# A gated mix of a state-space scan and an MLP on one core: W1 read and summed twice, scan allowed into the output stage, full-size b2 rows, x loaded first

## The chip, the cores and the metric

The kernel runs on one core of a Trainium2 chip. A core has engines that run side by side, each with its own queue in program order: TensorE (PE, matrix products, whose results go to eight banks of PSUM), VectorE (DVE), ScalarE (ACT), GpSimd (POOL) and SyncE (SP). SP, ACT and POOL also issue transfers (DMA) between the chip's main memory and the on-chip SBUF. Engines wait for one another through semaphores. The time is that of one execution on the device in microseconds (us), lower is better. Several executions give a median; one of them was taken with the hardware profiler.

## The reference

For x of 2048 rows and 1024 columns in bf16 (S rows, D columns), with F = 3584 hidden columns:

```python
x = A_x
g = sigmoid((x * gate_w).sum(-1, keepdims=True))
# A: diagonal complex state space, P = 1024 states
dt = exp(log_dt); Lam_bar = exp(dt * Lam)
B_bar = ((Lam_bar - 1) / Lam)[:, None] * (B_re + 1j * B_im)
Bu = einsum("bld,pd->blp", x, B_bar)
for t in range(L): h = Lam_bar * h + Bu[:, t]
a = 2 * einsum("blp,dp->bld", h, C_re + 1j * C_im).real + x * Dskip
# B: MLP on the layer-normed x
y = layernorm(x)
b = gelu(y @ w1 + b1) @ w2 + b2
return g * a + (1 - g) * b
```

## The kernel before, in words

**Matrix products with seven multiplications.** Every large product is done on 2 by 2 blocks with seven block products instead of eight. The class `SG` (L836) holds one such *group*: `p1` to `p7` are its seven products, each written by `mm` (L819) as a run of matmuls of 128 by 128 stationary and 128 by 512 moving operands (L828 where a bank is started, L830 where it is added to). Four of the seven use sums or differences of blocks. These are fp16 or bf16 tiles that DVE makes beforehand with `dve_tt` (L881 and L882), always in sets of four additions. Banks of PSUM are taken in rings: two for `p1`, two for `p5`, three for `p6`, so a bank comes round again two or three groups later.

**Stages on PE, in this order.** First x and B are transposed on PE (`t_x`, `t_b`) or by a transposing DMA, and the *bu* stage multiplies x by B, some of it plainly (`bu_plain`), the rest in groups (`bu_group`). Results go to the buffer `US` in main memory. The gate and the row sums of x come from a product with two columns (`z_gate`, L1024, bank 7). They are written to memory and read back in another layout (`z_move`, L1043), and layernorm (`ln_stats`) follows. Then come the MLP stages, eight of them: m(Fh,c) multiplies half c of the rows by half Fh of W1 and ends in gelu, and b(Fh,c) multiplies this by half Fh of W2. Their order is m(0,0), b(0,0), m(0,1), b(0,1), m(1,1), b(1,1), m(1,0), b(1,0) (L1465). The results of b, times (1 - g), are stored to or added into the buffer `ACS` in memory. The last stage, y, takes eight state blocks of 256 rows one after another, multiplies each by C (`y_group`, L1437), adds what `ACS` holds and the Dskip term, and stores the output.

**W1.** `w1_prep` (L1219) brings one 256-column block of W1 into one of four slots. Each half of W1 is used by two m stages. At the first use (m(0,0) and m(1,1)) the raw block is read, 512 KB in rows of 512 bytes, DVE makes the four sums (L1236 to L1239), and POOL stores block and sums together, 896 KB, to the buffer `W1S` (L1241). At the second use this is read back (L1225), with no work for DVE.

**b2.** In the b stages with Fh = 0 each group has two more matmuls that add b2. One has a stationary operand of one row of ones, the other of two rows (+1 and -1), against rows of b2 held in `B2B`: `v_one`, `v_sgn`, `v_b2l`, `v_b2r`. They are the only matmuls that read the tile `stg`.

**The scan.** `ssm` (L1120) does one *unit*: four blocks of 128 states by 256 rows. There are sixteen units. Each reads from `US`, multiplies by a table of rotations (L1142), combines (L1145), scans (L1156) and turns back, all on DVE, and stores to `HS`. Its buffers are three slots in `SSM` and two temporaries. It has the lowest priority on DVE (50) and so fills what the stages on PE leave. Units 8 to 15 finish state blocks 0 to 7.

**The y stage.** `y_load` (L1417) loads a state block (L1421), the rows of `ACS` (L1431) and of x (L1432), and has DVE multiply x by Dskip (L1433) and add it, times the gate, to the rows of `ACS` (L1434). `y_prep` makes the sums of the state block; `fin` makes the output from the banks (L1453 and L1455). The blocks come in the order 4, 5, 6, 7, 0, 1, 2, 3 (`YORD`). The places `H0` (states), `AV` (rows of `ACS`), `XV` (x) and `DB` (Dskip) lie in `SSM`, in the scan's tables `TABR` and in what hidden activations (`HT`) and W2 (`W2Q`) leave free. In particular the first two states lie in `SSM` and the first four rows of `ACS` in `TABR`, which the scan uses until it ends.

**What sets the order.** All work is entered as tasks with a priority and with dependences found from the memory that they read and write. A planner (`_schedule_once`) plays the tasks with modelled durations and writes one fixed order for each engine. At run time each engine executes its order and waits by semaphore. A task that waits holds up everything behind it on its engine.

Of the kernel before, what the change touches and what calls it, by code (L numbers as in the profile page):

```python
# [419 lines left out]
def build(nc, A_x, A_Lambda_re, A_Lambda_im, A_B_re, A_B_im, A_C_re, A_C_im, A_log_dt, A_Dskip,  # L420
# [6 lines left out]
    CH = 512  # L427
# [18 lines left out]
    with es:  # L446
# [194 lines left out]
        def t_x(k, prio):  # L641
            bk = tbank()
            v = XNAT[k]

            def em(e, k=k, bk=bk):
                ins = None
                base = XNAT[k].ap
                for dt in range(DT):
                    src = AR.v(XOFF(k) + dt * 256, [(1, 128)]).ap
                    ins = e.transpose(V(PS16[bk], dt * 128, [(1, 128)]), src, V(IDENT, 0, [(1, 128)]))  # L650
                return ins
            g.add("pe", 0.06 * DT, prio, em, reads=[v, b_ident], writes=[b_ps[bk]], name="xT_T%d" % k)
            o = AR.v(xqo(0, 0) + k * 256, [(512, DT), (1, 128)])
            first_e.append(g.add("dve", 0.65, prio, lambda e: e.tensor_copy(o.ap, V(PS16[bk], 0, [(128, DT), (1, 128)])),
                                 reads=[b_ps[bk]], writes=[o, b_ps[bk]], name="xT_e%d" % k))

        def t_b(pt, prio):
            s = pt % 4
            for ri in range(2):
                bk = tbank()  # L660

                def em(e, ri=ri, bk=bk):
                    ins = None
                    for dt in range(DT):
                        src = AR.v(RX + s * 4096 + ri * 2048 + dt * 256, [(1, 128)]).ap
                        ins = e.transpose(V(PS16[bk], dt * 128, [(1, 128)]), src, V(IDENT, 0, [(1, 128)]))
                    return ins
                g.add("pe", 0.06 * DT, prio, em, reads=[BN[pt], b_ident], writes=[b_ps[bk]], name="bT%d.%d" % (pt, ri))
                o = AR.v(bqo(pt, 2 * ri), [(1, D)])
                first_a.append(g.add("act", c_act(D), prio, lambda e, o=o, bk=bk: e.activation(o.ap, V(PS16[bk], 0, [(1, D)]), AF.Copy),  # L670
                                     reads=[b_ps[bk]], writes=[o, b_ps[bk]], name="bTe%d.%d" % (pt, ri)))

        load_b(0, (-0.95, 0))
# [5 lines left out]
        for k in range(4):  # L679
            t_x(k, (-0.8, k))  # L680
        t_b(0, (-0.79, 0))
        bk0 = tbank()
        g.add("pe", 0.06, (-0.75, 0),
              lambda e: e.transpose(V(PS16[bk0], 0, [(1, NROW)]), V(STG, 0, [(1, 128)], npart=NROW), V(IDENT, 0, [(1, NROW)], npart=NROW)),
              reads=[b_stg, b_ident], writes=[b_ps[bk0]], name="cst_T", extra=[g.tasks[-2]])
        g.add("pool", 0.4, P0,
              lambda e: e.affine_select(V(STG, 0, [(1, 128)], npart=2), V(ONESF, 0, [(1, 128)], npart=2), [[0, 128]], ALU.is_equal, -1.0,
                                        base=0, channel_multiplier=1),
              reads=[b_ones], writes=[b_stg], name="signs").slack = 4.0
        v_one = View(V(STG, 0, [(1, 128)], npart=1), [b_stg])  # L690
        v_sgn = View(V(STG, 0, [(1, 128)], npart=2), [b_stg])
# [324 lines left out]
        b_zs = B("zs")  # L1016
# [26 lines left out]
        def z_move():  # L1043
            prio = (1.0, seq[0])

            def em_st(e):
                return [e.dma_start(out=ZS[r].rearrange("(c t) -> c t", c=NCH), in_=bass.AP(AR.h[F32], r * zrow + ZR // 4, [[32 * zrow, NCH], [1, CH]])) for r in range(2)]
            g.dma(prio, em_st, 2 * L * 4, sem("d_zst", True), reads=[zr], writes=[b_zs], name="zst", ndma=2, q="pool").slack = 0.5

            def em_ld(e):  # L1050
                return [e.dma_start(out=C(("Z", "SUM")[r], 0, NTT), in_=bass.AP(ZS.tensor, ZS.offset + r * L, [[1, 128], [128, NTT]]), allow_slow_non_contiguous=True) for r in range(2)]
            g.dma(prio, em_ld, 2 * L * 4, sem("d_zl"), reads=[b_zs], writes=[bc("Z%d" % k) for k in range(NTT)] + [bc("SUM%d" % k) for k in range(NTT)], name="zl", ndma=2)
# [15 lines left out]
        for c in range(2):  # L1068
            if c == 1:
                z_gate(0)  # L1070
            for pt in range(2):
                bu_plain(pt, c)
# [4 lines left out]
        for n, (pt, pr) in enumerate(order):  # L1077
# [3 lines left out]
            if (pt, pr) == (0, 1):  # L1081
                z_gate(1)
                z_move()
                x_sums(1, seq[0])
# [35 lines left out]
        def ssm(pg, q):  # L1120
            s = nxt("sb", NSB)
            so, MA, MB = SB0 + s * 4096, TM0, TM0 + 4096
# [59 lines left out]
        v_b2l = AR.v(B2B, [(1, 512)], npart=1)  # L1182
        v_b2r = AR.v(B2B + 1024, [(1, 512)], npart=2)
# [35 lines left out]
        def w1_prep(j, first, q, ex=()):  # L1219
# [20 lines left out]
            ov = AR.v(o0, [(1, 3584)])  # L1240
            g.dma((10.0, q), lambda e: e.dma_start(out=W1S[j], in_=ov.ap), 128 * 7168, ssem("w1s", s, True), reads=[ov], writes=[b_w1s[j]], name="w1s%d" % j, q="pool")  # L1241
# [85 lines left out]
        def b_group(Fh, c, tp):  # L1327
# [8 lines left out]
            if Fh == 0:  # L1336

                st["A11"], mv["B11"] = st["A11"] + [v_one], mv["B11"] + [v_b2l]
                st["S1"], mv["T1"] = st["S1"] + [v_sgn], mv["T1"] + [v_b2r]
# [32 lines left out]
        H0 = [SSM, SSM + 8192] + [HT + 8192 * i for i in range(4)] + [SSM, SSM + 8192]  # L1372
        YR = HT + 49152
        AV = [TABR + 4096 * i for i in range(4)] + [YR + 4096 * i for i in range(4)]
        XV = [SSM + 16384, YR + 16384, YR + 18432, HT + 43008, HT + 45056]
        DB = SSM + 18432
# [4 lines left out]
        YORD = (4, 5, 6, 7, 0, 1, 2, 3)  # L1381
# [35 lines left out]
        def y_load(yi):  # L1417
# [3 lines left out]
            g.dma((52.0, yi), lambda e: e.dma_start(out=o.ap, in_=HS[qb]), 2 * UE * 128 * 2, ssem("hg", yi), reads=[b_hs[pg][qb] for pg in range(PG)], writes=[o], name="hg%d" % yi,  # L1421
                  extra=pe_last if yi > 2 else ())
            if yi == 0:
                g.dma((51.0, 0), lambda e: e.dma_start(out=v_db.ap, in_=bass.AP(A_Dskip.tensor, A_Dskip.offset, [[0, 128], [1, D]])), 128 * D * 2, sem("d_dskb"), writes=[v_db], name="dskb")
            for t in range(2):
# [3 lines left out]
                xi = 0 if n < 4 else 1 + n % 4  # L1429
# [3 lines left out]
                g.add("dve", c_tt16(D), (52.0, n), lambda e, xv=xv: e.tensor_tensor(xv.ap, xv.ap, v_db.ap, ALU.mult), reads=[xv, v_db], writes=[xv], name="xd%d" % k)  # L1433
                g.add("dve", c_dve(D), (52.0, n, 1), lambda e, xv=xv, av=av, k=k: e.scalar_tensor_tensor(av.ap, xv.ap, C("G", k), av.ap, ALU.mult, ALU.add),  # L1434
                      reads=[xv, av, bc("G")], writes=[av], name="xa%d" % k)

        def y_group(yi):  # L1437
# [5 lines left out]
            su, s5 = AR.v(YU[yi % 2], [(1, 512)], F32), AR.v(AO + 16384, [(1, 512)], F32)  # L1443
# [23 lines left out]
        for (kind, Fh, c) in blocks:  # L1467
            if kind == "m":
                for j in range(NP2):
                    w1order.append((Fh * NP2 + j, (Fh, c) in ((0, 0), (1, 1))))  # L1470
# [37 lines left out]
        for n, it in enumerate(flat):  # L1508
# [4 lines left out]
            if (kind, Fh, c, x) == ("b", 1, 0, 3):  # L1513
                y_load(0)
                y_load(1)
# [39 lines left out]
            if n == 0:  # L1555
                def em_b2(e):
                    return [e.dma_start(out=AR.v(B2B, [(1, D)], npart=1).ap, in_=bass.AP(B_b2.tensor, B_b2.offset, [[0, 1], [1, D]])),
                            e.dma_start(out=AR.v(B2B + 1024, [(1, 512)], npart=1, p0=1).ap, in_=bass.AP(B_b2.tensor, B_b2.offset, [[0, 1], [1, 512]]))]
                g.dma((40.0, 0), em_b2, 4096, sem("d_b2b"), writes=[v_b2l, v_b2r], name="b2b", ndma=2)
# [6 lines left out]
            if last_of_block:  # L1566
                if nit is None:
                    prev.p4()
                else:
# [13 lines left out]
                    else:  # L1583
# [5 lines left out]
                        prev.p4()  # L1589
                    prev = None  # L1590
# [53 lines left out]
```

## Time and profile before

| | us |
|---|---|
| median of 4 executions | 575.82 |
| lowest, highest | 574.67, 577.54 |
| the profiled execution | 574.67 |
| its span, first to last instruction | 572.9 |
| PE busy in the span | 552.1 |
| DVE busy in the span | 511.7 |

A row of the profile names line, engine, operation, what is written and read with its shape, and a count. "L828 PE MATMUL ps<-ar" is a matmul of line 828 that reads the large SBUF tile `ar` and writes PSUM. In the views in order of time the first number is the start and the second the length, both in us; a bracket gives the idle time before it and what ended it. A matmul's length includes its passage through the array and overlaps the next one, so the distance between starts is what it costs. In the page a row of groups gives the busy time, the mean of one in ns, and the idle time before them. PEld is the loading of the stationary operand. The granted clock of PE is 0.998 in this execution.

### The profile page before, as it was taken

The numbers are of one execution on the slowest core, as the hardware profiler recorded it, in microseconds if no ns is written. First come the engines' busy times: TensorE is split into PE (matmuls) and PEld (weight loads), VectorE is DVE, ScalarE is ACT, GpSimd is POOL, SyncE is SP. The second block draws the span as 40 slices with busy tenths as digits, with TensorE's granted clock in tenths as the row PEclk, the third lists the DMA queues.
The fourth block names the chain that finished last, engine by engine and source line by source line (L and its number), as shares of the span: only waits on it lengthen the run. The fifth ranks groups of instructions, "written<-read, shape, count | busy, mean of one in ns | idle before, by whom it ended". The sixth has DMA issues, their size and how long they took to land.

```text
span 572.9 us, 7432 instructions
## 1 busy us (share of the span) xinstructions
PE 552.1 (96%) x2569; PEld 249.0 (43%) x2617; DVE 511.7 (89%) x865; ACT 279.6 (49%) x465; POOL 98.8 (17%) x159
## 2 busy tenths in 40 slices
PE   5899999999999999999999999999999999999994
PEld 4444444444334444444434444444444444444442
DVE  3899999999999999999999999999995878998652
ACT  2978999667652247662236673336662322111110
POOL 0024856630101010001211000210000210011000
PEclk9999999999999999999999999999999999999999
DMA  8995999889994766403878999899669999777501
GB/s 273 234 285 111 286 298 317 276 286 288 373 256 127 262 244 228 146 33 114 263 295 295 336 286 212 212 276 258 199 144 255 305 311 281 246 246 265 180 37 55
DMA packets 116675, 134.50 MB, mean 235 GB/s; under 512 B 70548, under 2 KB 92565, under 8 KB 115614
## 3 DMA queue, kind: packets, MB, share of 16 engines
q1 hardware_dynamic: 102548, 79.72, 50.1%
q0 software_dynamic: 13952, 54.29, 29.6%
q8 instruction: 20, 0.33, 0.2%
q14 instruction: 17, 0.14, 0.1%
q10 hardware_dynamic: 138, 0.02, 0.0%
HBM read 63.48 MB, written 54.80 MB: 206 GB/s over the span
## 4 chain that ended last, share of the span: by engine, by line
PE 82%; DVE 11%; issue 2%; ACT 2%; DMA 1%; SPq 0%; DVEq 0%; ACTq 0%
PE ps L830 57%; PE ps L828 24%; DVE ar L882 4%; DVE ar L1142 2%; DVE ar L1275 2%; DVE ar L1156 1%; DVE ar L1145 1%; DMA ar<-in_A_x_dram 1%; ACT ar L670 1%; PE ps L1033 1%; PE ps L650 0%; DVE ar L1357 0%; ACT ar L912 0%; ACT L720 0%; DVE ar L968 0%
## 5 line engine op out<-in xcount | busy, mean ns | idle before, releaser
L830 PE MATMUL ps<-ar 128*128 128x512 f16 (+1 forms) x1683 | 389.9, 379 | 4.1 <-DVE ar L1357 1.0
L830 PEld LDWEIGHTS ps<-ar 128*128 128x128 f16 (+1 forms) x1720 | 166.3, 98 | 207.2 <-issue 4.4
L828 PE MATMUL ps<-ar 128*128 128x512 bf16 (+1 forms) x741 | 181.7, 379 | 1.4 <-DVE ar L882 0.8
L882 DVE TENSOR_TENSOR ar<-ar 128x512 f16<-128x512 bf16 (+7 forms) x216 | 139.9, 686 | 8.0 <-PE ps L828 3.4
L828 PEld LDWEIGHTS ps<-ar 128*128 128x128 bf16 (+1 forms) x752 | 72.6, 98 | 90.2 <-DVE ar L882 3.5
L1156 DVE TENSOR_TENSOR_SCAN ar<-cst,init,ar 128x256 bf16<-128x256 f32 x128 | 88.0, 735 | 0.4
L846 ACT ACTIVATE ar<-ps 128x512 f32<-128x512 f32 x100 | 58.9, 593 | 48.2 <-PE ps L828 33.2
L1142 DVE TENSOR_TENSOR ar<-ar 128x2048 bf16<-128x2048 bf16 x64 | 77.2, 1219 | 0.0
L854 ACT ACTIVATE ps<-ps 128x512 f32<-128x512 f32 x66 | 38.5, 583 | 71.8 <-PE ps L828 65.2
L1271 ACT ACTIVATE ar<-ps,cst 128x512 bf16<-128x512 f32 x56 | 38.4, 686 | 25.9 <-PE ps L830 25.4
L847 ACT ACTIVATE ar<-ps,cst 128x512 f32<-128x512 f32 x32 | 22.0, 687 | 56.6 <-PE ps L828 35.8
L1354 ACT ACTIVATE ar<-ps,cst 128x512 f32<-128x512 f32 x32 | 22.0, 687 | 46.1 <-PE ps L830 46.1
L1277 ACT ACTIVATE ar<-ar,cst 128x512 bf16<-128x512 f32 x56 | 40.0, 715 | 8.5 <-DVE ar L1275 8.4
L1145 DVE TENSOR_TENSOR ar<-ar 128x1024 bf16<-128x1024 bf16 x64 | 42.4, 686 | 0.2
L1275 DVE TENSOR_TENSOR ar<-ps,ar 128x512 f32<-128x512 f32 x56 | 38.3, 684 | 2.7 <-PE ps L830 2.2
L897 POOL DMA_DIRECT2D scr_u<-ar x32 | 25.1, 785 | 52.0 <-ACT ar L912 17.8
L1357 DVE SCALAR_TENSOR_TENSOR ar<-ps,cst,ar 128x512 f32<-128x512 f32 x32 | 23.9, 748 | 11.2 <-PE ps L830 11.1
L1455 DVE SCALAR_TENSOR_TENSOR ar<-ps,cst,ar 128x512 bf16<-128x512 f32 x32 | 23.8, 748 | 9.7 <-PE ps L830 9.6
L1366 POOL DMA_DIRECT2D scr_ac<-ar x16 | 13.8, 881 | 81.2 <-issue 32.9
L1364 POOL DMA_DIRECT2D scr_ac<-ar x16 | 8.5, 532 | 100.6 <-DVE ar L882 47.7
L1462 POOL DMA_DIRECT2D out_dram<-ar x14 | 7.6, 544 | 83.4 <-DVE ar L1455 83.4
L1174 POOL DMA_DIRECT2D scr_h<-ar x16 | 9.6, 600 | 66.9 <-DVE ar L1145 66.7
(105 smaller groups left out, 261.8 us busy)
## 6 DMA issues: line engine op xcount, KB each, us to landing
scr_ac<-ar POOLq DMA_DIRECT2D x32, 512.0 KB, 7.6
scr_w<-ar POOLq DMA_DIRECT2D x14, 896.0 KB, 6.5
ar<-scr_w SPq DMA_DIRECT2D x14, 896.0 KB, 6.0
ar<-in_A_x_dram SPq DMA_DIRECT2D x32, 256.0 KB, 5.1
scr_u<-ar POOLq DMA_DIRECT2D x32, 256.0 KB, 4.8
ar<-scr_u SPq DMA_DIRECT2D x16, 512.0 KB, 5.7
scr_h<-ar POOLq DMA_DIRECT2D x16, 512.0 KB, 7.2
ar<-scr_ac SPq DMA_DIRECT2D x16, 512.0 KB, 7.3
```

The source lines that it names most:

```text
L828: ins = e.matmul(V(PS[bk], 0, [(1, n)]), st[i].ap, mv[i].ap, start=(i == 0), stop=(i == K - 1))
L830: ins = e.matmul(V(PS[bk], 0, [(1, n)]), st[i].ap, mv[i].ap, start=False, stop=(i == K - 1), skip_group_check=True)
L846: return e.activation(o.ap, V(PS[bk], 0, [(1, 512)]), AF.Copy)
L854: g.add("act", c_act(512), (pb[0], q - 2), lambda e: e.activation(V(PS[b], 0, [(1, 512)]), V(PS[a], 0, [(1, 512)]), AF.Copy), reads=[b_ps[ ...
L882: g.add("dve", c_tt16(n), (pb[0], q), lambda e: e.tensor_tensor(o.ap, a.ap, b.ap, op), reads=[a, b], writes=[o], name=nm, extra=ex).slack ...
L897: g.dma((1.0, q), lambda e: e.dma_start(out=US[pt // 4, :, 4 * pr:4 * pr + 4, r0:r0 + T], in_=evv.ap), 2 * 128 * CH * 2, ssem("us", 2 * ks ...
L1142: g.add("dve", c_tt16(UE), pri(i), lambda e: e.tensor_tensor(o.ap, a.ap, tbl.ap, ALU.mult), reads=[a, tbl], writes=[o], name=nm + tag)
L1145: g.add("dve", c_tt16(UE // 2), pri(i), lambda e: e.tensor_tensor(o.ap, a.ap, b.ap, op), reads=[a, b], writes=[o], name=nm + tag)
L1156: lambda e, pt=pt, ri=ri, vin=vin, go=go: e.tensor_tensor_scan(go.ap, Cb("R", pt, T), vin.ap, V(INIT, pt * 2 + ri, [(1, 1)]), ALU.mult, AL ...
L1271: g.add("act", c_act(512, ap_operands=1), (10.0, q + 1), lambda e: e.activation(o.ap, V(PS[bk], 0, [(1, 512)]), AF.Gelu_apprx_tanh, bias=C ...
L1275: g.add("dve", c_dve(512), (10.0, q - 2), lambda e: e.tensor_tensor(sv.ap, V(PS[bk], 0, [(1, 512)]), sv.ap, ALU.add), reads=[b_ps[bk], sv] ...
L1277: g.add("act", c_act(512, psum=False, ap_operands=1), (10.0, q + 3), lambda e: e.activation(o.ap, sv.ap, AF.Gelu_apprx_tanh, bias=C("B1", ...
```

## The change

- **x first.** The loads of x's first two blocks go out ahead of B's; B's real and imaginary halves are loaded by separate tasks (`load_b0`) between and behind the blocks of x. The transposes on PE follow the same order, in an order fixed by dependences, with banks of their own.
- **Full-size b2 rows.** The sign tile has 128 rows (row 0 is 1, the others -1), and `B2B` is cleared on POOL before b2 is loaded into its rows 0 and 1, so that the two matmuls of b2 have full-size operands.
- **The gate in halves.** `z_move` stores and reads back each half of the rows as soon as its `z_gate` is done.
- **W1.** Every use reads the raw block and makes the four sums; the store to `W1S` is gone.
- **Scan and y.** Units 13 and 15 use a buffer in the tables of the first eight units, and unit 14 the third slot, so that two slots of `SSM` come free after unit 12. `H0`, `AV`, `XV` and `DB` get new places. `YORD` becomes 4, 5, 6, 0, 1, 2, 3, 7. At the start of the last W2 group only the first state block and Dskip are loaded; the rows of `ACS` and x for the first block, and everything for the second, are entered after that group's last product. The Dskip work gets priority 49 (52 before), ahead of the scan. The intermediate `s5` gets two places in turn.

```diff
+        load_b0(0, A_B_re)
+        load_b0(1, A_B_im)
+        BN[0] = AR.v(RX, [(1, 2 * D)])
         for k in range(4):
             load_x(k, (-0.9, k))
...
+        t_x(0, (-0.8, 0), 7, [])
+        t_x(1, (-0.8, 1), 3, last_pe())
+        t_b(0, (-0.8, 2), (0,), (1, 2), last_pe())
+        t_x(2, (-0.8, 3), 0, last_pe())
+        t_x(3, (-0.8, 4), 7, last_pe())
+        t_b(0, (-0.79, 0), (1,), (1, 2), last_pe())
+        bk0 = 3
...
-              lambda e: e.affine_select(V(STG, 0, [(1, 128)], npart=2), V(ONESF, 0, [(1, 128)], npart=2), [[0, 128]], ALU.is_equal, -1.0,
+              lambda e: e.affine_select(V(STG, 0, [(1, 128)]), V(ONESF, 0, [(1, 128)]), [[0, 128]], ALU.is_equal, -1.0,
...
             if c == 1:
                 z_gate(0)
+                z_move(0)
...
         def ssm(pg, q):
-            s = nxt("sb", NSB)
-            so, MA, MB = SB0 + s * 4096, TM0, TM0 + 4096
+            un = pg * NQ + q
+            s = nxt("sb", NSB) if un < 13 else 2 + un % 2
+            so, MA, MB = (SB0 + s * 4096 if s < 3 else TABR + 4096), TM0, TM0 + 4096
...
-        v_b2l = AR.v(B2B, [(1, 512)], npart=1)
-        v_b2r = AR.v(B2B + 1024, [(1, 512)], npart=2)
+        v_b2l = AR.v(B2B, [(1, 512)])
+        v_b2r = AR.v(B2B + 1024, [(1, 512)])
+        v_b2 = AR.v(B2B, [(1, D)])
...
-            ov = AR.v(o0, [(1, 3584)])
-            g.dma((10.0, q), lambda e: e.dma_start(out=W1S[j], in_=ov.ap), 128 * 7168, ssem("w1s", s, True), reads=[ov], writes=[b_w1s[j]], name="w1s%d" % j, q="pool")
...
-                st["A11"], mv["B11"] = st["A11"] + [v_one], mv["B11"] + [v_b2l]
+                st["A11"], mv["B11"] = st["A11"] + [v_sgn], mv["B11"] + [v_b2l]
...
-        H0 = [SSM, SSM + 8192] + [HT + 8192 * i for i in range(4)] + [SSM, SSM + 8192]
         YR = HT + 49152
-        AV = [TABR + 4096 * i for i in range(4)] + [YR + 4096 * i for i in range(4)]
-        XV = [SSM + 16384, YR + 16384, YR + 18432, HT + 43008, HT + 45056]
-        DB = SSM + 18432
+        H0 = [SSM] + [HT + 8192 * i for i in range(4)] + [SSM, HT, HT + 8192]
+        AV = [YR + 4096 * i for i in range(4)] + [AO + 2048, AO + 10240, TABR + 8192, TABR + 12288]
+        XV = [TABR, YR + 16384, YR + 18432, HT + 43008, HT + 45056]
+        DB = B2B
...
-        YORD = (4, 5, 6, 7, 0, 1, 2, 3)
+        YORD = (4, 5, 6, 0, 1, 2, 3, 7)
...
-                    w1order.append((Fh * NP2 + j, (Fh, c) in ((0, 0), (1, 1))))
+                    w1order.append((Fh * NP2 + j, True))
...
             if (kind, Fh, c, x) == ("b", 1, 0, 3):
-                y_load(0)
-                y_load(1)
+                y_load(0, ())
...
+                g.add("pool", 0.8, (39.0, 0), lambda e: e.memset(v_b2.ap, 0.0), writes=[v_b2], name="b2z")
                 g.dma((40.0, 0), em_b2, 4096, sem("d_b2b"), writes=[v_b2l, v_b2r], name="b2b", ndma=2)
...
                         prev.p4()
+                        if nk == "y":
+                            y_load(0, (0, 1), False)
+                            y_load(1)
```

## The prediction

> **What bounds the kernel now.** I began with the page's sums and its 40 slices (14.3 us each; a digit is the busy share in tenths).
>
> ```profile
> PE 552.1 (96%) x2569; PEld 249.0 (43%) x2617; DVE 511.7 (89%) x865; ACT 279.6 (49%) x465; POOL 98.8 (17%) x159
> PE   5899999999999999999999999999999999999994
> DVE  3899999999999999999999999999995878998652
> ```
>
> PE is full from the third slice to the last but one, and DVE nearly so until slice 30: PE sets the end, with DVE close behind. What can be won is time in which PE stands or steps slowly. In PE's timeline I took starts against starts: a 512-column matmul normally follows the last by 0.216 us (2,321 of 2,568 steps; a step of 0.43 is one record missing). The longer steps lie in three places.
>
> First the beginning, PE's timeline and then ACT's:
>
> ```profile
> 5.51 1.03 PE L650 MATMUL ps<-ident,ar 128*128 128x128 bf16 x8 [5.51 <-DMA ar<-in_A_x_dram]
> 7.05 2.85 PE L650 MATMUL ps<-ident,ar 128*128 128x128 bf16 x24 [0.50 <-DMA ar<-in_A_x_dram]
> 9.81 1.63 PE L666 MATMUL ps<-ident,ar 128*128 128x128 bf16 x16
> 11.94 0.21 PE L684 MATMUL ps<-ident,stg 76*128 76x76 bf16 x1 [0.50 <-ACT ar L670]
> 12.20 1.67 PE L828 MATMUL ps<-ar 128*128 128x512 bf16 x7
> ...
> 23.30 1.89 PE L1033 MATMUL ps<-ar,gwc 128*2 128x512 bf16 x16 [1.42 <-DVE ar L768]
> ```
> ```profile
> 10.86 1.94 ACT L670 ACTIVATE ar<-ps 128x1024 bf16<-128x1024 bf16 x2 [6.06 <-PE ps L666]
> 22.09 1.06 ACT L670 ACTIVATE ar<-ps 128x1024 bf16<-128x1024 bf16 x1
> ```
>
> PE waits for x, whose loads stand behind both halves of B's first block; the first real product starts at 12.20. The wait before 23.30 is named DVE, but the gate's product takes bank 7, and ACT empties it until 23.15: ACT ends that wait.
>
> Second, one b2 product of the sixteen (start, length):
>
> ```profile
> 183.25 1.46 PE L828 MATMUL ps<-ar 128*128 128x512 bf16 x6
> 184.64 0.38 PE L828 MATMUL ps<-ar,stg 1*128 1x512 bf16 x1
> 184.96 1.25 PE L830 MATMUL ps<-ar 128*128 128x512 f16 x5
> ```
>
> The step into it is 0.312 us and out of it 0.317, not 0.216.
>
> Third, stalls by stage, from the table by stage (length; busy PE, PEld, DVE, ACT, POOL; clock; DMA share; GB/s). The rows are m(0,0), m(0,1), m(1,1), m(1,0), b(1,0), y:
>
> ```profile
> 120.80:163.80 43.00, 41.95 (x188) 17.87 (x190) 42.84 (x68) 30.15 (x49) 5.28 (x9) 1.00 0.99 307
> 207.80:252.00 44.20, 43.89 (x202) 19.91 (x204) 42.53 (x65) 29.90 (x49) 2.12 (x4) 1.00 0.52 187
> 294.00:342.00 48.00, 46.20 (x211) 20.45 (x213) 47.30 (x75) 30.68 (x50) 5.25 (x10) 1.00 0.95 301
> 383.00:430.00 47.00, 46.48 (x214) 20.96 (x216) 45.95 (x71) 31.43 (x52) 3.27 (x6) 1.00 0.79 204
> 430.00:467.50 37.50, 37.34 (x172) 17.00 (x174) 27.55 (x34) 11.47 (x17) 5.69 (x7) 1.00 1.09 285
> 467.50:566.60 99.10, 97.77 (x447) 44.32 (x453) 76.38 (x103) 14.79 (x25) 8.83 (x16) 1.00 0.62 204
> ```
>
> Summing PE's long steps (b2's own excess left out): 1.8 us in m(0,0), 0.2 in m(0,1), 2.1 in m(1,1), 0.5 in m(1,0), 0.5 elsewhere after 25 us, none in b(1,0) and y. The two expensive stages are those that make W1's sums, also W2's sums, at a DMA share near 1.
>
> **x first.** The queue SP issues in order, 0.4 to 0.5 us each; before, the first six landings were 3.7, 4.3 (B), 5.5, 7.0, 7.7, 8.3 (x). The order becomes x0, x1, B re, x2, x3, B im. Giving these the same landings: x0's transposes begin at 3.7; B re is turned at 5.6 and copied by ACT until 7.5, before only until 11.8; x3 lands 7.7, B im 8.3; B im turned by 9.1; the constants' transpose follows in bank 3 with no wait for ACT (0.5 before). First product at about 9.4: 2.8 earlier. From there ACT's copies (one second-long copy per half of each of three more B blocks, as before) run about 11 us to the gate: 20.4 against 23.3. The other B blocks landed at 12.4 and transposed x at 16.5, so neither holds it. Ends: -1.0 if B's later blocks set ACT's pace, -3.0 if all of it arrives; I take **-2.6**, near what the landings give. PE has no stall over 0.27 from 25 to 120, so the shift arrives.
>
> **Full-size b2 rows.** Sixteen products, 0.096 in and 0.101 out: 16 x 0.197 = **-3.15**, all on PE. The Trainium skill ("TensorE: Matmul & The Clock Gate", *LDWEIGHTS* and the table of *Why this matters for your kernels*) speaks against it: a weight load's time goes by its columns and not its rows, and one matmul of few rows takes as long as a full one. By that the gain is 0; the row shows each alone is not shorter (0.38 us), but the steps around it are longer. I take the row, and keep 0 for the high end. The cost: one memset on POOL (204 ns was measured for 128x128), some 40 us before its use; nothing.
>
> **The gate in halves.** Two stores of 0.6 more on POOL, two loads of 0.6 more on SP. Between 40 and 50 us POOL is a quarter busy (2.68 of 10); the first half moves to about 25 us, where x's loads are queued on SP and could stand behind its load by up to 2.6 us (the old transfer's wait). They were issued from 24.1 and are wanted for layernorm, not by PE before 73.9: 0. Layernorm's first half may start earlier; PE never waited for it: 0.
>
> **W1's sums again.** 14 blocks more, four DVE additions each. One set took 1.47 us from start to start (1.56 busy at 127.77): 14 x 1.47 = **20.6 us of DVE**, half in m(0,1), half in m(1,0), ahead of the scan in priority, so the scan is what moves. It ended at 426 with its last store issued at 429.2; it would end near 447 plus what b(1,0) itself asks (DVE 27.5 of 37.5), so about 460. The cover: 9.95 us of idle DVE in b(1,0), 22.7 in y. 10.7 us are left for y, and some 2 us of Dskip work done before 467 move there too: 12.7 of 22.7. Only the last state block comes from the last scan unit, and it is now used last, at about 550; the others end by 440. So capacity suffices; without own buffers and order the 10.7 would stand before y.
> What can't be hidden is lateness: DVE runs in order, and a set behind a scan multiply (1.22) is late by that much. The nearest rows are the stages that have sets: 1.8 and 2.1 against 0.2 and 0.5. As much again would be +3.2; but the worst waits there stood behind W2's sums (two of 3584 elements took 2.35 at 148.09) and behind L1357, not a set alone. I take **+1.4** (0 to +4).
>
> **W1's stores gone, second reads smaller.**
>
> ```profile
> scr_w<-ar POOLq DMA_DIRECT2D x14, 896.0 KB, 6.5
> ar<-scr_w SPq DMA_DIRECT2D x14, 896.0 KB, 6.0
> ar<-in_B_w_dram SPq DMA_DIRECT2D x14, 512.0 KB, 6.3
> ```
>
> The 25 MB of the first two rows become 7.3 MB; a read takes as long. In m(0,0) a load took 10.8 us at worst, and POOL stood 15.0 for one with stores behind it. What waits for a store is the next load into its slot, which waits for the products too, and those end later: **-0.5** (0 to -1.5), by less crowding.
>
> **Into y.** The x and partial-sum loads for the first y blocks go into W2's place, so not before W2's last products, from 460 on, where four loads were already under way by 441. With 7.3 to landing the first is there at about 472; its use is the y block's first output at 476. If it is late, PE feels it only when the block after next (12.1 us each) takes that bank again, at 491. Moved with these loads: nine issues on SP (0.5 each), past nothing but the third block's, and beside two 512 KB stores of the last W2 group. The second state block (7.6) finds its place free after that group's first product and is used at 480; the third goes out at 473 as its place comes free, is used at 491. **+0.4** (0 to +6).
>
> **Sum** against the profiled execution, 574.67 (572.9 span, 1.8 around it): -2.6 - 3.15 + 1.4 - 0.5 + 0.4 = -4.45, 570.2. The median of the four is 575.82, 1.15 higher: **571.4**. About 0.3% (1.7 us) is what a measurement of this kernel can tell from no change: faster begins at 574.1, slower at 577.5.
>
> **Rivals.**
> - *The second sums come late* (slower). Place: DVE in m(0,1) and m(1,0). Each set stops PE by a good part of a scan multiply, 0.6 us: 8.4 instead of 1.4, 578.4. Break-even with the 5.65 gained and 0.5 and 0.4 netted is 0.41 a set; slower by 0.3% from 0.53. For it: DVE has 0.2 to 1.7 us idle per such stage. Against: m(0,0) and m(1,1) paid 0.28 a set, all causes together.
> - *The start doesn't shift*: x first, but ACT and B's later blocks set the gate's time; -0.5 instead of -2.6, and the sums 2.0 instead of 1.4: 574.1. For it: ACT is busy 9.25 of 10 us from 20 to 30. Against: it idles 6.06 before 10.86.
> - *The crowding was the cause of the stalls*: stores gone, sums hidden; m(0,0) and m(1,1) lose 3 of 3.9: 567.5. For it: the DMA share 0.99 and 0.95 there. Against: the longest wait, 1.0 at 298.29, is put down to DVE.
> - *The switch to y stalls*: late loads hold DVE in order, the sums of the next state behind them; +6: 577.
>
> **How the numbers follow.** Forecast 0.60 (own range 568.5 to 573.8), late sums 0.14, no shift 0.10, crowding 0.11, switch 0.05. Faster: 0.60 + 0.11 and half of no shift, 0.76; same: half of no shift and a third of the two slow ones, 0.11; slower 0.13. Range: 567.5 takes in crowding; above, I stop at 577.0, which leaves out most of the late sums.
>
> **What would show it.** First real product near 9.4 and the gate near 20.4; steps around b2 of 0.216; L1241's stores gone and 56 more additions; scan ending about 455 to 465 with y's first outputs not late; PE stalls in m(0,1) and m(1,0) of about 1.4 more together. It is wrong if those reach 6 us, if y has gaps over 1 us, or if b2's steps stay at 0.31.

## The result: no difference that can be measured

The changed kernel takes 576.54 us (median of 35 runs, 570.92 to 582.44), the kernel before on the same calls 575.35 (56 runs). The ratio is 0.9997, with a 95% interval of 0.9982 to 1.0012. The forecast was 571.4, a clear gain. Ratios here compare fast executions only, while the medians take in all of a kernel's executions, so the two part where a kernel has many slow ones (`start_only` below most of all).

The profiled execution of the changed kernel took 577.18 us (span 575.4) against 574.67 (572.9): 2.5 more. Its page, engine sums and the slices (14.4 us each) of PE and DVE:

```profile
PE 550.3 (96%) x2569; PEld 251.1 (44%) x2617; DVE 529.7 (92%) x921; ACT 278.5 (48%) x465; POOL 89.7 (16%) x148
PE   6999989889999999999999999999999999999985
DVE  4999889999999999999999999999999979999942
```

DVE has 18.0 us more work in 56 more instructions, as the change adds it. It is now full from slice 34 to 38, where it was at 8, 9, 9, 8, 6 before. PE has 1.8 us less work, yet its slices 6, 8 and 9 have fallen from 9 to 8.

The two early gains arrived. PE's timeline after, at the start and around one b2 product (start, length):

```profile
3.57 1.89 PE L649 MATMUL ps<-ident,ar 128*128 128x128 bf16 x16 [3.57 <-DMA ar<-in_A_x_dram]
...
9.71 1.67 PE L839 MATMUL ps<-ar 128*128 128x512 bf16 x7 [0.53 <-DVE cst L704]
...
19.33 1.89 PE L1044 MATMUL ps<-ar,gwc 128*2 128x512 bf16 x16
...
184.14 1.46 PE L839 MATMUL ps<-ar 128*128 128x512 bf16 x6
185.44 0.38 PE L839 MATMUL ps<-ar,stg 128*128 128x512 bf16 x1
185.65 1.67 PE L841 MATMUL ps<-ar 128*128 128x512 f16 x7
```

The first product starts at 9.71 (12.20 before) and the gate's at 19.33 (23.30), with no wait ahead of it. The b2 product lies 0.22 from the one before and 0.21 from the one after, where it was 0.31 and 0.32.

What ate them is in PE's waits after (total, times, longest) and in PE's timeline at the places of the largest ones:

```profile
PE ps L841 <- ACT ar L857: 4.3, 2, 2.5
PE ps L839 <- DVE ar L893: 2.5, 4, 1.1
PE ps L839 <- DMA ar<-scr_h: 2.4, 1, 2.4
```
```profile
77.71 1.90 PE L841 MATMUL ps<-ar 128*128 128x512 bf16 x8 [2.54 <-ACT ar L857]
...
103.85 1.90 PE L841 MATMUL ps<-ar 128*128 128x512 bf16 x8 [1.77 <-ACT ar L857]
...
503.68 1.90 PE L839 MATMUL ps<-ar 128*128 128x512 f16 x8 [1.11 <-DVE ar L893]
...
551.17 3.51 PE L839 MATMUL ps<-ar 128*128 128x512 bf16 x8 [2.42 <-DMA ar<-scr_h]
```

Summed from PE's start-to-start steps in both traces, beside the terms of the forecast (us, after less before). A stall is here the part of a step over 0.216, so it is somewhat longer than the idle time in the brackets:

| where | forecast | measured |
|---|---|---|
| start, to the gate's product | -2.6 | -4.0 |
| sixteen b2 products | -3.15 | -3.15 |
| first products, 53 to 120 us: stalls 0.27 before, 4.66 after | 0 | +4.4 |
| sums made twice: m(0,1), m(1,0) | +1.4 | -0.1 |
| stores gone: m(0,0) +0.5, m(1,1) -1.8 | -0.5 | -1.3 |
| W2 blocks b(0,0), b(0,1) and b(1,1) | 0 | +0.8 |
| output stage y: stalls 4.4, half clock about 1.6 | +0.4 | +6.0 |
| sum | -4.45 | +2.65 |

The measured sum is 0.1 to 0.2 off the difference of the two profiled executions. The miss is 7.1 us. Two rows, the first products and the output stage, are 10.0 over their forecast; the others are together 2.9 better than theirs.

**The first products.** The wait at 77.71 begins at DVE. DVE's timeline after, then ACT's:

```profile
74.52 0.42 DVE L893 TENSOR_TENSOR ar<-ar 128x512 f16<-128x512 bf16 x1 [4.03 <-DMA ar<-in_A_B_im_dram]
74.86 0.69 DVE L979 TENSOR_TENSOR ar<-ar 128x512 bf16<-128x512 f32 x1
```
```profile
75.63 0.60 ACT L977 ACTIVATE ar<-ps 128x512 f32<-128x512 f32 x1 [2.96 <-PE ps L841]
```

DVE, which takes its work in order, stands 4.03 us for a sum of blocks of B, until the transposing load of B im has landed. Behind it stands an addition on a finished product (L979, until 75.55). ACT's wait is named PE, but the product had been done since 75.18: the wait instruction at the head of ACT's queue, begun at 71.84, was released at 75.56, by L979. Then come ACT's L977, L807 and the copy that PE needs (L857, until 77.66), and PE goes on at 77.71.

That load of B im was issued at 60.5 and landed at 74.5; the last one went out at 64.9 and landed at 80.7. Before the change the last pair landed at 72.3 and 74.7. In that time the packets take long on average: from 66 to 68 us the 256-byte packets of the transposing loads 66 ns and the 4 KB packets of the stores on POOL's queue 617, where means of 22 to 34 and 160 to 170 are seen in the quicker stretches around it. But the median stays at 18 and 173 ns. A few packets stand very long, and they end together: 19 packets of 256 bytes that began within 0.05 us of 65.46 took 1.20 to 1.23 us each, and fifteen of 4 KB that began from 67.8 to 68.3 all ended at 69.7 to 69.8. So the transfers stop for 1 to 2 us at a time more than they run slowly. The DMA engines count as busy all that time, for a fraction of the bytes.

The wait at 103.85 stands behind ACT, which waits 1.56 us for DVE and then loads the table for the tanh at 101.80 (1.28 us) ahead of the copy that PE needs.

**The last state block.** Views of after: DVE's timeline, POOL's, then the chain of work that ended last:

```profile
472.57 1.28 DVE L1453 SCALAR_TENSOR_TENSOR ar<-ar,cst 128x1024 f32<-128x1024 bf16 x1 [2.35 <-DMA ar<-scr_ac]
...
502.34 0.69 DVE L1163 TENSOR_TENSOR ar<-ar 128x1024 bf16<-128x1024 bf16 x1
...
536.29 0.69 DVE L1163 TENSOR_TENSOR ar<-ar 128x1024 bf16<-128x1024 bf16 x1
```
```profile
541.66 1.20 POOL L1481 DMA_DIRECT2D out_dram<-ar  x2 [9.96 <-DVE ar L1474]
542.85 0.54 POOL L1192 DMA_DIRECT2D scr_h<-ar  x1
```
```profile
542.85 3.36 DMA scr_h<-ar
546.26 4.86 DMA ar<-scr_h
```

The scan has the lowest priority on DVE. From 470 to 480 DVE stands 4.5 us in order for rows of `ACS` and x whose loads take 11 to 15 us, with the rest of the last unit behind it; this rest comes from 495.5 to 503.0. Its very last addition (L1163, 0.69 us long) comes 33 us later still, at 536.29. The store is ready at 537.0, then stands 5.9 us in POOL's queue behind two stores of the output, which wait for DVE too, goes out at 542.85, lands at 546.2; the load lands at 551.1, and PE has stood for 2.4 us. The windows of the output stage of after (length; busy PE, PEld, DVE, ACT, POOL; clock; DMA share; GB/s):

```profile
480.00:490.00 10.00, 9.80 (x46) 4.33 (x45) 9.96 (x15) 1.62 (x3) 0.57 (x1) 1.00 0.91 364
...
530.00:540.00 10.00, 9.95 (x47) 4.55 (x47) 10.00 (x15) 1.57 (x3) 0.98 (x2) 1.00 0.37 107
540.00:550.00 10.00, 8.70 (x40) 3.78 (x39) 7.45 (x11) 1.19 (x2) 2.26 (x5) 1.00 0.55 190
550.00:560.00 10.00, 8.78 (x33) 3.68 (x35) 4.00 (x6) 1.21 (x3) 0.43 (x1) 0.83 0.18 72
```

DVE is full from 480 to 540 and has room only from about 545 on, after the last addition was due. In the window of PE's wait the granted clock is 0.83: for some 3.4 us a matmul follows the last by 0.427 us, not 0.216.

### The profile page after: what moved, and what is told of

Its sections match the earlier page's. It is cut to its first block, busy times and chain, and to the rows that moved or that the text cites. A ratio compares the mean times of both kernels' runs of the same rounds, so it can differ in the third digit from the quotient of the medians.

```text
span 575.4 us, 7467 instructions
## 1 busy us (share of the span) xinstructions
PE 550.3 (96%) x2569; PEld 251.1 (44%) x2617; DVE 529.7 (92%) x921; ACT 278.5 (48%) x465; POOL 89.7 (16%) x148
## 4 chain that ended last, share of the span: by engine, by line
PE 72%; DVE 17%; DMA 5%; issue 4%; ACT 1%; POOL 0%; SPq 0%; DVEq 0%; ACTq 0%
PE ps L841 49%; PE ps L839 21%; DVE ar L893 5%; DMA ar<-in_A_x_dram 2%; DVE ar L1453 2%; DVE ar L1160 2%; DVE ar L1474 2%; DVE ar L1293 2%; DVE ar L1452 1%; DVE ar L1472 1%; DMA ar<-scr_h 1%; DVE ar L1163 1%; DMA ar<-in_A_B_re_dram 1%; PE ps L665 1%; DVE ar L1174 1%
## 5 line engine op out<-in xcount | busy, mean ns | idle before, releaser
L893 DVE TENSOR_TENSOR ar<-ar 128x512 f16<-128x512 bf16 (+8 forms) x272 | 161.8, 631 | 8.8 <-DMA ar<-in_A_B_im_dram 4.0
L857 ACT ACTIVATE ar<-ps 128x512 f32<-128x512 f32 x100 | 58.6, 593 | 50.9 <-PE ps L839 38.6
L1163 DVE TENSOR_TENSOR ar<-ar 128x1024 bf16<-128x1024 bf16 x64 | 43.0, 686 | 0.3
L1474 DVE SCALAR_TENSOR_TENSOR ar<-ps,cst,ar 128x512 bf16<-128x512 f32 x32 | 23.9, 749 | 9.8 <-PE ps L841 9.7
L1453 DVE SCALAR_TENSOR_TENSOR ar<-ar,cst 128x1024 f32<-128x1024 bf16 x16 | 20.2, 1281 | 2.4 <-DMA ar<-scr_ac 2.4
```

Of the source, the lines that this page charges most:

```text
L857: return e.activation(o.ap, V(PS[bk], 0, [(1, 512)]), AF.Copy)
L893: g.add("dve", c_tt16(n), (pb[0], q), lambda e: e.tensor_tensor(o.ap, a.ap, b.ap, op), reads=[a, b], writes=[o], name=nm, extra=ex).slack ...
L1163: g.add("dve", c_tt16(UE // 2), pri(i), lambda e: e.tensor_tensor(o.ap, a.ap, b.ap, op), reads=[a, b], writes=[o], name=nm + tag)
L1474: g.add("dve", c_dve(512), (10.0, q), lambda e: e.scalar_tensor_tensor(o.ap, V(PS[bk], 0, [(1, 512)]), C("G", k), a.ap, ALU.mult, ALU.add) ...
```

## The experiments

My theory after the result had three parts. The start's gain is lost to crowded transfers in the first 120 us, because an earlier start is planned into another order. The gate in halves adds to that. And DVE's shortage stands before the last state block. The rivals: x first or the b2 rows bring nothing; the second sums of W1 come late in the middle stages; the stalls have other causes, so that undoing a part moves nothing. Each kernel's orders are planned anew, so a part that is undone can also move transfers elsewhere. "Before" was 575.1 to 575.6 us on all these calls. Ratios are to it, with 95% intervals.

**1. The early gains alone.** `start_b2` is the kernel before with x first and the full-size b2 rows; `start_only` has x first alone, `b2_only` the rows alone.

> The kernel before with x loaded first and full-size b2 rows, nothing else. Theory A (both early gains are whole, and the other parts eat them): the gate's product at 19.3 us instead of 23.3 and the b2 steps at 0.216, so 575.4 - 4.0 - 3.15 = 568.3 us, 567 to 570. Rival R1 (the earlier start itself runs into B's transposing loads and the stalls from 50 to 130 us come with it): 571 to 575.

> The kernel before with x loaded first alone. Theory D (in this plan, four us earlier, the transfers of 73 to 105 us fall into a stretch of slow packets, as in the run of both early parts): a wait of some 8 us near 99 us and the half clock after it, 581.9 + 3.15 = 585 us, 581 to 588. If the b2 part has a share in it: 571 to 576.

> The kernel before with full-size b2 rows alone. Its plan of the engines' orders is otherwise that of the kernel before. Theory A: sixteen products lose 0.197 us each, 575.1 - 3.15 = 572.0 us, 571.3 to 572.7. Rival (the time returns as waits on DVE in m(1,1)): 573 to 575.

| kernel | median us (runs) | ratio |
|---|---|---|
| `start_b2` | 581.89 (10) | 1.0078 (1.0041 to 1.0115) |
| `start_only` | 582.99 (21) | 1.0073 (1.0048 to 1.0097) |
| `b2_only` | 573.28 (22) | 0.9974 (0.9956 to 0.9992) |

x first, which takes 4 us off the start, makes the kernel slower by 0.7%. `start_b2` came out above both of its expectations. Its PE waits, PE's timeline, and the windows around the place:

```profile
PE ps L841 <- ACT ps L865: 10.6, 2, 7.8
```
```profile
99.52 6.49 PE L841 MATMUL ps<-ar 128*128 128x512 f16 x16 [7.80 <-ACT ps L865]
```
```profile
90.00:95.00 5.00, 1.72 (x8) 0.59 (x6) 0.00 (x0) 1.63 (x3) 0.00 (x0) 1.00 1.31 124
95.00:100.00 5.00, 0.48 (x2) 0.21 (x3) 2.65 (x5) 2.66 (x6) 1.07 (x2) 0.51 1.10 160
100.00:105.00 5.00, 5.00 (x13) 1.69 (x12) 4.37 (x10) 3.67 (x7) 2.45 (x4) 0.50 1.18 221
```

At 90 to 95 us DVE and POOL do nothing, the DMA share is 1.31 and 124 GB/s move. In flight are, among others, two stores of u (issued 78.8 and 79.6, landed 91.4 and 97.3), the first W1 store (83.1, landed 100.3) and a transposing load of layernorm's result (78.6, landed 101.3). The 256-byte packets from 85 to 100 us take 82 ns on average (median 18). PE stands for 7.8 us; the clock is at half from 95.1 to 105.4, and PE works in the last 5.8 us of this. The rows alone bring 1.5 us by the ratio and 2.0 by the medians, of their 3.15: in their profile PE gained a wait of 1.7 us in y (behind ACT's L845) that the kernel before has not.

**2. Holding one group of loads.** `start_b2_hold` is `start_b2` with W1's first loads held until the transposing loads of layernorm's result have landed:

```
+        xl = [t for t in g.tasks if t.name.startswith('xnT0')]
         for _ in range(4):
-            w1_next(0)
+            w1_next(0, xl)
```

> The kernel before with x first and full-size b2 rows, as in the first run of these two, and W1's first loads held until layernorm's transposing loads have landed, so that W1's first store doesn't fall among them. Theory D: without that overlap the packets stay at their usual time, the 8 us wait near 99 us goes, 568 to 573. If the transposing loads and the stores of Bu alone bring it: 576 to 583.

571.55 us (8 runs), 0.9931 (0.9907 to 0.9955): 8.5 us under `start_b2` by the ratios, 10 by the medians. The stalls from 53 to 120 us go from 8.6 us to 0.28, and the mean of the 256-byte packets from 85 to 100 us from 82 ns to 28. So both early gains are real, and what hid them lay in the transfers of this stretch. By the spans of the profiled executions they are worth 5.5 us (572.9 less 567.4), which is the 7.1 of the start and the rows less some 2 us of stalls more in the middle stages; by the medians 3.7 and by the ratio 4.0.

**3. The gate.** `z_whole`: the changed kernel with the gate moved as a whole (`z_move` once, as before).

> The changed kernel with the gate stored and read back whole, as before. Theory B (the gate in halves brings layernorm's stores forward, and they crowd the transposing loads of B, which landed at 74.5 and 80.7 us): the wait of 2.7 us at 77.7 us goes, perhaps those at 103.9 and 127.9 too: 570 to 573 us. If the halves do nothing: 575.5 to 576.5.

573.38 us (13), 0.9966 (0.9949 to 0.9983). The stalls from 53 to 120 us are 1.83 instead of 4.66, those in y stay at 4.33. Layernorm's four stores go out at 64.2 to 69.5 us, instead of 59.6 to 62.8, and B im lands at 67.3 and 70.4, instead of 74.5 and 80.7. The halves cost 2 us by the ratios and 3 by the medians; they do it by the order that they give, since PE never waits for the gate itself.

**4. The sums of W1 and the last state block.** `w1_stored` is the changed kernel with W1's sums stored and read back as before. `half_w1` makes them twice for the first half of W1 only. `last_unit` keeps all of them twice and gives the scan's last unit a better priority:

```
-            return (50.0, un, i)
+            return (50.0 if un < 15 else 48.0, un, i)
```

> The changed kernel with W1 and its sums stored at the first use and read back at the second, as before; 28 + 28 additions fewer on DVE. Theory C (the 20 us of additions push the last scan unit so far that the last state block comes late): the wait before the last y block and the half clock after it go, some 4.4 us: 571 to 573, stalls from 50 to 130 us stay. Rival R2 (the additions are late at every use, as my prediction feared): the stalls of m(0,1) and m(1,0) were 0 and 0.6 in the changed kernel's profile, so no more than 0.6 comes from there.

> The changed kernel, with the last scan unit (the sixteenth) put ahead of the Dskip work in priority (48 instead of 50), so that it isn't left until its state block is due. Theory C: its store goes out near 480 us instead of 543, the wait of 2.4 us before the last y block and the 3.4 us at half clock (1.7 lost) go: about 4 us less than the changed kernel, 571 to 573. If the last y block's wait is only where an earlier delay shows: 575 to 577.

> The changed kernel with the sums made again only for the first half of W1, in m(0,1); those for m(1,0) are stored and read back as before. Half of the additional DVE work, 10 us, and none of it within 80 us of the y stage. Theory C (DVE's cover before the last state block is due is about 10 us): no stall over 1 us in y, 571 to 573. If any second making costs (DVE late in m(0,1)): 573 to 576. The stalls of 50 to 130 us, 5 to 6 us in the changed kernel, are outside of this and may change either way with the plan.

| kernel | median us (runs) | ratio | stalls in y, us |
|---|---|---|---|
| changed | 576.54 (35) | 0.9997 (0.9982 to 1.0012) | 4.4 |
| `w1_stored` | 571.10 (6) | 0.9930 (0.9908 to 0.9952) | 0.0 |
| `half_w1` | 571.54 (7) | 0.9924 (0.9889 to 0.9960) | 0.8 |
| `last_unit` | 574.51 (22) | 0.9985 (0.9965 to 1.0005) | 5.4 |

Windows of `w1_stored` in y; then of `last_unit` PE's timeline, DVE's, and a piece of the chain of work that ended last:

```profile
530.00:540.00 10.00, 10.00 (x49) 4.49 (x47) 6.91 (x11) 1.18 (x2) 1.08 (x2) 1.00 0.47 159
540.00:550.00 10.00, 10.00 (x48) 4.58 (x47) 6.39 (x10) 1.18 (x2) 1.08 (x2) 1.00 0.14 52
```
```profile
490.50 3.27 PE L841 MATMUL ps<-ar 128*128 128x512 f16 x8 [4.92 <-DVE ar L1474]
```
```profile
475.12 1.29 DVE L1163 TENSOR_TENSOR ar<-ar 128x1024 bf16<-128x1024 bf16 x2
...
485.06 2.62 DVE L893 TENSOR_TENSOR ar<-ar 128x1024 f16<-128x1024 bf16 x4 [4.68 <-DMA ar<-scr_h]
```
```profile
470.12 14.92 DMA ar<-scr_h
```

With seven sets of sums fewer (`half_w1`) or fourteen (`w1_stored`) the scan ends at 464.7 and 424.8, not at 537.0, and PE stands little or not at all in y. With the last unit first it ends at 476.4, with no set fewer, and the wait at 551 is gone as well. So what makes that wait is the late end of the last unit, and this came of the order as much as of the quantity of DVE work. But `last_unit` has a new wait: PE stands 4.9 us at 490.50 for DVE's output operation (L1474). DVE is not behind the scan there, which ended 14 us earlier; it stands 4.7 us, in order, for the sums of a state block whose load took 14.9 us (470.1 to 485.0). In the changed kernel that load is as slow (469.5 to 484.5), but DVE has other work until then. The expected 571 to 573 was missed by this, and against the changed kernel no difference shows beyond the noise. Not run were a kernel that brings forward the one addition at 536.29, and one that takes its store out from behind those of the output. By the trace each had room for the 2.4 us: 33 us passed before that addition, and its store stood 5.9 us.

In m(0,1) and m(1,0) the second sums cost nothing in any of these traces (0 to 0.66 us of stalls), so the rival that they come late there falls.

**5. The crowd at 60 to 75 us.** In the changed kernel four stores of layernorm's result go out between 59.6 and 62.8 us, beside the two slow loads. `xn_held` holds these stores until B's last loads have landed; `half_w1_xn_held` is `half_w1` with the same wait, `half_w1_hold` is `half_w1` with the hold of experiment 2.

```
-  ... name="xns%d" % k, q="pool")
+  ... name="xns%d" % k, q="pool",
+      extra=[t for t in g.tasks if t.name.startswith("bTd7")])
```

> The changed kernel with one wait added: the stores of layernorm's result (line 1021, scr_xn) start only after B's last transposing loads have landed; in the changed kernel four of them are issued between 59.6 and 62.8 us, while two transposing loads of B im are under way that take 14.0 and 15.8 us (usually about 6 to 8). Theory (these stores are the crowd that slows the transposing loads' packets, which makes PE stand 2.7 us at 77.71): the 256-byte packets go back to about 25 ns, B im lands by about 70, the stalls from 53 to 120 us fall from 4.66 to about 2 (the 1.9 behind ACT stay), the time to about 573.5. Rival (the stores of u, scr_u, crowd it, or the onset has nothing to do with the layernorm stores): packets stay at 40 ns on average, no change, 576.5. The stalls in y of 4.4 us stay by both.

> The same wait put into the kernel whose W1 sums are made twice for the first half of W1 only. Theory (the two causes, crowded loads in the first 120 us and DVE's shortage before the last state block, are separate and add up): half_w1 has 2.27 us of stalls from 53 to 120, of which about 1.5 go, so 571.54 becomes about 570. Rival (they are not separate, because every new wait gives the planner another order and another pile-up): anything from 570 to 576, without a link to the loads of B.

> The kernel whose W1 sums are made twice for the first half of W1 only, with W1's first four loads held behind the transposing loads of layernorm's result (the hold that took start_b2 from 581.89 to 571.55). Theory (W1's first loads crowd whatever lies from 80 to 100 us): half_w1 had its W1 load at 82.7 already, and its stalls there are small, so the hold is worth at most 1 us: 571 (570 to 572). Rival (the loads at 60 to 75 us are the crowd, which the hold does not touch): no change, 571.5. It is worse if W1 then comes late for m(0,0): PE stalls at 120 to 128 us of over 2.5 more, 574.

| kernel | median us (runs) | ratio | stalls 53 to 120 us |
|---|---|---|---|
| `xn_held` | 572.07 (10) | 0.9931 (0.9907 to 0.9955) | 0.28 |
| `half_w1_xn_held` | 569.55 (6) | 0.9886 (0.9853 to 0.9918) | 3.14 |
| `half_w1_hold` | 572.97 (9) | 0.9935 (0.9903 to 0.9968) | 5.41 |

The longest of PE's waits after its first one, of `xn_held` and then of `half_w1_xn_held`:

```profile
PE ps L839 <- DMA ar<-scr_h: 2.7, 1, 2.7
```
```profile
PE ps L841 <- ACT ps L865: 2.3, 1, 2.3
```

One wait added on these stores makes the changed kernel faster by 3.8 us by the ratios and 4.5 by the medians. The stalls from 53 to 120 us fall by 4.4 us; the waits in y stay. B im lands at 70.1 and 70.8 instead of 74.5 and 80.7.

Both cures together give the fastest kernel of the study, 1.1% under the kernel before. That they add up is likely but not shown. The two ratios taken together would give 0.9858, and 0.9886 was measured; but the interval reaches from 0.9853 to 0.9918 and overlaps with that of `half_w1`. Nor is the gain in the place where I looked for it. B im lands at 68.8 and 69.6 us and the wait at 77 is gone, yet a wait of 2.3 us behind ACT has come at 100, and the stalls before 120 us are 3.14 where `half_w1` has 2.27.

The hold that was worth 8.5 us in `start_b2` is worth nothing measurable in `half_w1`, and its profile even has 5.41 us of stalls before 120: there the crowd lies at 60 to 75 us, where the hold doesn't reach, and the 256-byte packets take 42 ns on average.

What these runs don't settle is why the transfers stop. `w1_stored` has the same four stores and two loads within 0.6 us of the same times. Windows of after, then of `w1_stored`:

```profile
66.00:68.00 2.00, 2.00 (x11) 0.92 (x10) 1.97 (x6) 1.75 (x4) 1.17 (x2) 1.00 1.13 79
68.00:70.00 2.00, 1.95 (x10) 0.88 (x9) 2.00 (x6) 1.55 (x5) 0.80 (x2) 1.00 0.86 111
```
```profile
66.00:68.00 2.00, 2.00 (x11) 0.88 (x9) 1.97 (x7) 1.75 (x5) 1.68 (x3) 1.00 1.08 390
68.00:70.00 2.00, 2.00 (x11) 0.90 (x10) 2.00 (x6) 2.00 (x5) 0.79 (x2) 1.00 1.13 258
```

Nearly the same traffic moves 79 GB/s in the one and 390 in the other; `w1_stored` has its slow stretch too (104 GB/s from 64 to 66 us), but it ends after 2 us. In `xn_held` a slow stretch is left as well (69 GB/s from 66 to 68), yet fewer transfers stand in it. So moving the stores away cures the stall; that the stores start the slowness is not shown.

**6. Without own buffers and order.** `noP5` has x first, the b2 rows, the gate in halves and all sums twice, but the scan's buffers, the loads, the priority of the Dskip work and the order of y as before.

> The changed kernel without its fifth part: x first, full b2 rows, the gate in halves, W1's sums made twice with none stored, but the scan's buffers, the loads and the order of the output stage as before. It shows what the own buffers and the block order cover. Theory (DVE's shortage before the last state blocks is what limits, the sums made twice are 20.6 us of DVE and the scan cannot run into the output stage): the output stage starts late and waits for the scan about 10 to 20 us, 590 (583 to 598). Rival (the sums hide in b(1,0)'s 9.95 us of idle DVE and in the small gaps of the other stages, so the fifth part was not needed): 574 or less.

601.21 us (6), 1.0401 (1.0357 to 1.0446). DVE's timeline at the end of the scan, then PE's at the first product of y:

```profile
464.70 1.29 DVE L1161 TENSOR_TENSOR ar<-ar 128x1024 bf16<-128x1024 bf16 x2
476.44 1.90 DVE L1449 TENSOR_TENSOR ar<-ar 128x1024 bf16<-128x1024 bf16 x3 [10.44 <-DMA ar<-in_A_Dskip_dram]
```
```profile
454.63 5.99 PE L841 MATMUL ps<-ar 128*128 128x512 bf16 x26
486.12 5.17 PE L839 MATMUL ps<-ar 128*128 128x512 bf16 x16 [25.51 <-DMA ar<-scr_h]
```

This is slower than the expected 583 to 598. The scan ends at 466.0 (429.0 before), PE is through with W2 at 460.6, and y starts at 486.1. The chain of waits between: the row of Dskip goes into the scan's room and can be issued only at 464.7, takes 11.65 us to land among the other loads, DVE uses it for 3.1 us, and the state block stands on SP behind an x load that waits for that: 479.9 to 486.0. So of PE's 25.5 us about 4 pass until the scan frees the room at 464.7, and some 21 go by the loads that were held up. The own buffers, the priority and the block order of the full change together keep these 25.5 us off PE; which of them does it was not run.

## Why the prediction was wrong

**"PE has no stall over 0.27 from 25 to 120, so the shift arrives"** is the first step that failed (+4.4 us). That no stall was seen in the trace of before says only that the loads were in time with *that* order of transfers. The kernel's order is planned from due times; shift the start by 4 us and other stores and loads fall together. `start_only` shows it in the purest form: the gain there is a loss of 0.7%. I had weighed only the transfers that the edit itself moves, and the rival "the start doesn't shift" looked at the wrong place: the start did shift, by more than I said.

**"Capacity suffices"** is the second (+0.4 forecast, 6.0 measured). The total was right: 20.6 us were forecast, 18.0 measured in DVE's busy time, and the scan ended at 466.0 where it can't run into y (`noP5`), against "about 460". (The start of that sum, a scan ending at 426, is the start of its last multiply; its last addition ends at 429.0.) The error was to count y's 22.7 us of idle DVE over the whole stage. The trace of before, parted at 535, about when the last store must be ready:

```profile
467.50:535.00 67.50, 67.18 (x308) 30.64 (x313) 58.13 (x78) 11.23 (x19) 6.13 (x11) 1.00 0.80 260
535.00:566.60 31.60, 30.59 (x141) 13.68 (x140) 18.25 (x26) 3.55 (x6) 2.70 (x5) 1.00 0.24 84
```

Until 535 DVE idles 9.4 us, where 12.7 were to be moved in. `w1_stored` shows the same: 0.1 us is idle from 490 to 520, and 12.6 from 530 to 560. A stage-long sum of idle time is a capacity only for work that may end with the stage. I had named the block and its due time ("used last, at about 550") and then didn't count idle time up to it.

Two more things were put at nothing in the term "Into y". Time in which DVE stands in order for a late load is no room either: the loads were taken at 7.3 and 7.6 us, took 11 to 15, and DVE stood 4.5 us for them in the changed kernel. And the new order of priorities, Dskip work ahead of the scan, leaves the scan's last addition behind the work of y, and its store behind the output's. `last_unit` shows that the scan can end at 476.4 with the same sums, so the shortage of room is not by itself the cause of the wait at 551.

**The second sums**, the rival that I gave most chance (0.14), cost nothing in the stages where they are made (-0.1 against +1.4, and against 8.4 in the rival).

**x first** was under-sized, -4.0 against -2.6: with B re copied at 7.03 instead of 10.86 the ACT copies ahead of the gate were done in time, and its wait of 1.42 went as well. **The b2 rows** were right in the trace to 0.05 us. The Trainium skill ("TensorE: Matmul & The Clock Gate", *LDWEIGHTS*), by which the load of one row costs no less than that of 128, would have given 0; the row decided, and rightly. **The stores gone** were worth 1.3 us in place of 0.5. **The gate in halves**, forecast at 0 with "PE never waited for it", cost 2 to 3 us through the order (`z_whole`).

**The rival "the switch to y stalls"** had the right size, 6 us, and in part the right mechanism: late loads did hold DVE in order at the switch (4.5 us from 470 to 480). But PE paid later, at 503.68 and 551.17, and not for the next state's late load alone; that the size agrees is partly luck. Its chance of 0.05 was too low. The measured 576.54 lies inside the whole range, 567.5 to 577.0, only because its upper end was set by this rival's 577; it is outside the forecast's own range of 568.5 to 573.8. One slip without effect: the "5.65 gained" in the break-even should be 5.75 (2.6 + 3.15).

## What to carry to other kernels

A gain at the start of a planned kernel is not kept by the absence of stalls after it: check what falls together once everything is 4 us earlier, above all transposing loads, and try a hold on one group of transfers before giving the gain up. Count idle time of an engine only up to the moment when the work must be done, and not over the stage in which it lies, and leave out what it spends standing in order for a load. When work of the lowest priority feeds a deadline, follow its last instruction and its store through the queues. When two parts of a change cancel, run each alone: here one wait and half of the second sums turned no change into a gain of 1.1%.

## What the runs showed of the hardware

Transfers came to a stop for 1 to 2 us at a time under nearly the same traffic that elsewhere ran through. In the changed kernel 19 packets of 256 bytes stood 1.20 to 1.23 us from 65.46 on, and fifteen of 4 KB stood until 69.7; the median packet took 18 and 159 to 185 ns from 62 to 72 us. In `w1_stored` there was one such stop, 21 packets of over 1 us at 64.5. Means (66 and 617 ns from 66 to 68 us) make of this a general slowness, which it is not. The DMA share was 1.08 in `w1_stored` with 390 GB/s and 1.13 in the changed kernel with 79, so it isn't a measure of what is moved.

PE's clock fell to half around waits of 2.34 us (`half_w1_xn_held`, 100.07), 2.42 (551.17), 4.92 (`last_unit`) and 7.80 (`start_b2`), but not after 2.34 in `half_w1_hold` (77.47), 2.54 (77.71) or 2.65 (`z_whole`, 546.80). So from 2.3 to 2.7 us the length of the wait alone doesn't decide. The half clock lasted 3.41 us at 551.17 and in `last_unit`, 6.83 in `start_only`, 10.24 in `start_b2` and 23.89 in `noP5`: once, twice, three and seven times 3.41. The Trainium skill ("TensorE: Matmul & The Clock Gate", *What's actually happening*) puts the fall after an idle window of about 3.4 us and notes that the window runs free. The lengths agree with such a window; a whole one of idling was not needed, since a wait of 2.34 us was enough. The 3.41 us at half clock add about 1.7 us to the wait at 551.17.
